# Seven tiles of scores a pair for the row maxima instead of eight, and another order of the prelude, in an attention and FFN kernel

## The chip, the cores and the metric

The kernel runs on one core of a Trainium2 chip. The metric is the device time of one execution in microseconds (us). A slot is one turn of the main loop, and a pair is two attention heads that are worked on together. Names such as PE (TensorE), DVE (VectorE), ACT (ScalarE), POOL (GpSimd) and SP (SyncE, whose queue issues all DMAs here) are those of the profile.

## What is computed

```python
q_n, k_n = rmsnorm(q, g_q), rmsnorm(k, g_k)          # 8 batches, 12 heads, 448 tokens, 64 wide
scores = matmul(q_n, k_n^T) / sqrt(64)
scores = scores - max(scores, axis=-1)
attn = exp(scores); attn = attn / (sum(attn) + 1e-9)
x = (attn @ v) laid out as 3584 tokens x 768
h = x @ w_in                                          # 768 x 2048
out = (s * relu(h)**2 + b) @ w_out                    # 2048 x 768
```

## The kernel before, in words

The 96 heads are 48 pairs (`NPAIR`), six pairs a batch. Each number is carried as a high part, rounded to the float32r type, and a low part, the rest, so that a product takes several float32r matmuls. Of a pair's tensors, `ka` holds the high part of the keys in partitions 0 to 63 (`D` = 64) and the low part in 64 to 127, and `qa` the high part of the queries twice, so one matmul of `qa` with `ka` gives nearly exact scores. `kb` and `qb` hold what is left over, and partition 64 of `qb` holds the shift, minus the maximum of each query's scores, which the second score matmul adds to the scores. Any shift near the maximum gives the same softmax, as numerator and sum are scaled alike.

The main loop (from line 895) runs over slots from `FIRST` = -22 to 384 and a few more; a pair has 8 slots (`W`), 4 for each head j, one for each block of keys. Slot s does, on each engine in the order written: the transposed scores of slot s (`score_t`, L434 and L437), two FFN matmuls, the exponential (`exponent`), then what `begun` generators have left, then the jobs that `at(slot, function, ...)` put into this slot, then the score of slot s+10 for the maxima (`score`, L396), more FFN matmuls, its maximum on DVE (`maximum`, L407), the late jobs (`convert`, `convert_out`, `invert`), and the product with the values of slot s-2 (`weigh`, L493). All engines and the SP queue take their instructions strictly in this written order.

Each of a pair's eight scores for the maxima has 112 queries, every fourth one (`c=NQ`, four columns of 112 rows), as weights against all 448 keys of its head. `shift` moves the maxima of one head by a DMA into the row of `qb`; `double_kb` copies the high keys into `kb` by a DMA.

Pairs 0 to 8 (`NR` = 9) get q and k from rows: `load_rows` (L251), `norm_rows` (ACT square L257, DVE sum L262, POOL L265 to L267), `turn` (PE transposes, L274), `split_turned` (ACT L282 to L284, DVE L286 and L287). Later pairs come by `load_kq`, `scale` and `split_kq` (ACT L377 and L378, POOL L380 and L381). `norm_rows` runs at slot s1-20, `turn` at s1-13, `split_turned` at s1-12 and its DVE half one slot later, with s1 = 8p + 4j. `double_kb` runs at s1-10 and `shift` at s1-6.

The weights `w_in` come as 64-bit floats in 24 pieces, `load_piece` (L129), and are converted by `convert` in five steps from the slots of `PACE`: DVE L133, L136, L138, L141, ACT L134 and L144, POOL L147.

During the first batch (slots 0 to 55) there is no FFN work. From slot 56 on each slot also holds six matmuls of the first FFN product (`filler`, L204) of the batch before, 288 for the 48 slots of a batch. After the last slot follow the rest of the first FFN product and the second one (L825).

Of the kernel before, what the change touches and what calls it, by code (L numbers as in the profile page):

```python
# [9 lines left out]
F32 = mybir.dt.float32  # L10
F32R = mybir.dt.float32r
I32 = mybir.dt.int32
AF = mybir.ActivationFunctionType
ALU = mybir.AluOpType
AX = mybir.AxisListType
# [14 lines left out]
FIRST = -22  # L30

FILL = (2, 2, 2)

PACE = (-18, -10, *range(1, 61, 5), *range(59, 89, 3))

GAP = 2

STEPS = {0: 2, 1: 3, 2: 4, 3: 5, 5: 6, 6: 7, 8: 8, 9: 9, 11: 10, 12: 11, 13: 12}

OUT = (92, *range(110, 141, 6), *(48 * b + i for b in range(3, 8) for i in range(14, 43, 7)))  # L40

# [2 lines left out]
def attention_then_relu2_ffn(  # L44
# [30 lines left out]
    V, S, G, T = nc.vector, nc.scalar, nc.gpsimd, nc.tensor  # L75

    NPAIR, P, _, SEQ = kq.shape
# [4 lines left out]
    D = P // 2  # L82
    NP = NPAIR // B
    H = 2 * NP
    TILES = 2 * SEQ // P
    NV = 2 * NP
    NR = rows0.shape[0]
    NQ = 4
    QC = SEQ // NQ
# [8 lines left out]
    W = 8  # L98
# [137 lines left out]
    lp = last.enter_context(tc.tile_pool(name="lpool", bufs=1, side="right"))  # L236
    ap = early.enter_context(tc.tile_pool(name="apool", bufs=1))
    if True:
        raws, kqs, invs, vrs, nmxs, shs, tks = ({} for _ in range(7))
        sts, movers, avs, uzs, zts, zbs, us = ({} for _ in range(7))  # L240
# [12 lines left out]
        def norm_rows(p, j):  # L253
            raw = raws[p, j].rearrange("p t c d -> p (t c) d")
            n = 2 * NQ
            sq = lp.tile([QC, n, D], F32, tag="al", bufs=2, name=f"sq{p}_{j}")
            S.activation(  # L257
                sq.rearrange("p i d -> p (i d)"), raw.rearrange("p i d -> p (i d)"), AF.Square
            )
            yield  # L260
            ssq = ap.tile([QC, n], F32, tag="ssq", bufs=2, name=f"ssq{p}_{j}")
            V.tensor_reduce(out=ssq, in_=sq, op=ALU.add, axis=AX.X)  # L262
            yield
            ri = ap.tile([QC, n], F32, tag="ri", bufs=2, name=f"ri{p}_{j}")
            G.tensor_scalar(ri, ssq, 1.0 / D, 1e-6, ALU.mult, ALU.add)  # L265
            G.tensor_tensor(ri, ri, mhalf[:QC, :n], ALU.pow)
            G.tensor_tensor(raw, raw, ri.unsqueeze(2).broadcast_to([QC, n, D]), ALU.mult)  # L267
# [11 lines left out]
        def split_turned(p, j):  # L279
            n, a = p % 2, slice(j * SEQ, (j + 1) * SEQ)  # L280
            (k, k_bank), (q, q_bank) = (tks.pop((p, j, t)) for t in range(2))
            S.copy(ka[n][:D, a], k)  # L282
            S.activation(qa[n][:D, a], q, AF.Copy, scale=gqk[:D])
            S.activation(qa[n][D:, a], q, AF.Copy, scale=gqk[:D])  # L284
            yield
            V.tensor_tensor(ka[n][D:, a], k, ka[n][:D, a].bitcast(F32), ALU.subtract)  # L286
            V.scalar_tensor_tensor(  # L287
                qb[n][:D, a], q, gqk[:D], qa[n][:D, a].bitcast(F32), ALU.mult, ALU.subtract
            )
            free.extend((k_bank, q_bank))  # L290
# [5 lines left out]
        def warm_up(n):  # L296

            to, bank = psum("warmth")
            for _ in range(n):
                T.matmul(to[:, :P], ident, ident, start=True, stop=True)  # L300
            free.append(bank)
# [61 lines left out]
        ka = [ap.tile([P, 2 * SEQ], F32R, name=f"ka{n}") for n in range(2)]  # L363
        qa = [ap.tile([P, 2 * SEQ], F32R, name=f"qa{n}") for n in range(2)]
        kb = [ap.tile([P, 2 * SEQ], F32R, name=f"kb{n}") for n in range(2)]
        qb = [ap.tile([P, 2 * SEQ], F32R, name=f"qb{n}") for n in range(2)]
        for t in qb:
            G.memset(t[D:P].bitcast(F32), 0.0)
        for t in kb:
            G.memset(t[D:P].bitcast(F32), 0.0)  # L370
            G.memset(t[D : D + 1].bitcast(F32), 1.0)

        def split_kq(p, j):

            t, n = kqs.pop((p, j)), p % 2
            a = slice(j * SEQ, (j + 1) * SEQ)
            S.copy(ka[n][:, a], t[:, 0])  # L377
            S.copy(qa[n][:, a], t[:, 1])  # L378
            yield
            G.tensor_tensor(ka[n][D:, a], t[D:, 0], ka[n][D:, a].bitcast(F32), ALU.subtract)  # L380
            G.tensor_tensor(qb[n][:D, a], t[:D, 1], qa[n][:D, a].bitcast(F32), ALU.subtract)  # L381

        def move(to, of):
            nc.sync.dma_start(to.bitcast(F32), of.bitcast(F32))
# [5 lines left out]
        def score(i):  # L390

            p, c = divmod(i, W)
            j, c = divmod(c, NQ)
            sh, bank = psum(f"sh{i}")
            a = slice(j * SEQ, (j + 1) * SEQ)
            T.matmul(  # L396
                sh[:QC, :SEQ], qa[p % 2][:, a].rearrange("k (p c) -> k c p", c=NQ)[:, c],
                ka[p % 2][:, a], start=True, stop=True,
            )
            shs[i] = sh, bank  # L400

        def maximum(i):
            p, c = divmod(i, W)
            if c == 0:
                nmxs[p] = ap.tile([QC, W], F32R, tag="nmx", bufs=2, name=f"nmx{p}")
            sh, bank = shs.pop(i)
            V.tensor_reduce(  # L407
                out=nmxs[p][:, c : c + 1], in_=sh[:QC, :SEQ], op=ALU.max, axis=AX.X, negate=True
            )
            free.append(bank)  # L410

        def shift(p, part):

            to = qb[p % 2][D : D + 1, part * SEQ : (part + 1) * SEQ]
            move(
                to.rearrange("o (p c) -> o p c", c=NQ), nmxs[p][:, part * NQ : (part + 1) * NQ]
            )
            if part:
                nmxs.pop(p)

        def chunk(i):
            p, g = divmod(i, W)
# [96 lines left out]
        def divide(p, step):  # L519

            if step == 1:
                nc.sync.dma_start(z_d[p].rearrange("j (p c) -> (j p) c", c=TILES), zts.pop(p))
            elif step == 2:
                zb = zbs[p] = lp.tile([P, SEQ], F32, tag="zb", name=f"zb{p}")
                for j in range(2):
                    nc.sync.dma_start(
                        zb[j * D : (j + 1) * D], z_d[p][j : j + 1].broadcast_to([D, SEQ])
                    )
            else:
                zb = zbs.pop(p)  # L530
                u = us[p] = lp.tile([P, SEQ], F32, tag="u", bufs=NP, name=f"u{p}")
                for j in range(2):
                    a = slice(j * D, (j + 1) * D)
                    G.tensor_tensor(u[a], uzs.pop((p, j))[a], zb[a], ALU.mult)  # L534
# [96 lines left out]
        def at(s_, f, *a):  # L631
            jobs[s_].append((f, a))

        for p in range(NPAIR):
            s0 = W * p
            if p >= NR:
                at(s0 - 32, load, p)
                at(s0 - 28, norm, p)
                at(s0 - 24, keep, p)
            for j in range(2):  # L640
                s1 = s0 + 4 * j
                if p >= NR:
                    at(s1 - 19, load_kq, p, j)
                    at(s1 - 19, spread, p, j)
                    at(s1 - 15, scale, p, j)
                    at(s1 - 13, split_kq, p, j)
                else:
                    at(max(s1 - 28, FIRST), load_rows, p, j)
                    at(s1 - 20, norm_rows, p, j)
                    at(s1 - 13, turn, p, j)  # L650
                    at(s1 - 12, split_turned, p, j)
                at(s1 - 10, double_kb, p, j)
                at(s1 - 6, shift, p, j)
                at(s1 + 6, take, p, j)
                at(s1 + 7, gather, p, j)
            at(s0 - (9 if p >= NV else 5), load_v, p)
            if p >= NV:
                at(s0 - 3, split_v, p)
            at(s0 + 13, invert, p)
            at(s0 + 14, divide, p, 1)  # L660
            at(s0 + 16, divide, p, 2)
            at(s0 + 18, divide, p, 3)
        for b in range(B):
            for g in range(NP):
                at(end(b + 1) - (2 if b < B - 1 else 4) + g, split_x, b, g)
        for _ in range(2):
            at(FIRST + 1, load_piece)
        for s_ in PACE:
            for n in range(5):
                at(s_ + n, convert, n)  # L670
# [218 lines left out]
        with tc.manual_schedule(engines=ORDERED):  # L889
            begun = []  # L890
            for s_ in range(FIRST, NSLOT + LAST + 2):
# [4 lines left out]
                    )  # L896
                for f, *of in drain.get(s_ - NSLOT, ()):
                    f(*of)
                if s_ == FIRST:
                    nc.sync.dma_start(gg, g_qk)  # L900
                    V.scalar_tensor_tensor(gqk, gg[:, 0:1], D**-0.5, gg[:, 1:2], ALU.mult, ALU.mult)
                if s_ == 0:
                    for t, x in ((sb_s, s), (sb_b, b_)):
                        nc.sync.dma_start(t, x.rearrange("(o d) -> o d", o=1).broadcast_to([P, 1]))
                if s_ == FIRST:
                    warm_up(30)
                if within(s_):
                    score_t(s_)
                filler(FILL[0])
# [40 lines left out]
            for n in range(NFC - 2):  # L950
# [4 lines left out]
                if n in STEPS:  # L955
                    k = STEPS[n]
# [86 lines left out]
```

## Time and profile before

| | us |
|---|---|
| median of 3 runs | 1417.05 |
| lowest and highest run | 1415.51, 1417.28 |
| the profiled execution, whole | 1414.78 |
| its span in the profile | 1412.3 |
| PE busy in the span | 1383.9 |
| DVE, POOL, ACT busy in the span | 1051.4, 1034.5, 867.5 |

The profiled execution is 2.27 us under the median, and 2.48 us of it lie outside the span. The busy shares are averages over three stages that are limited by different engines, so the text below reads them by stretches of time: the views by windows give, for each stretch, the busy time of each engine and in brackets its instructions.

### The profile page before, as it was taken

To read this page: it belongs to the slowest core of one execution; us is meant where nothing else is said; L and a number is where in the kernel's file an instruction comes from. 1 tells how busy PE (TensorE), PEld (TensorE's weight loads), DVE (VectorE), ACT (ScalarE), POOL (GpSimd) and SP (SyncE) were. 2 spreads that over 40 slices of the span, in tenths; PEclk is the share of its full clock that TensorE was granted. 3 is DMA by queue.
4 is the path that set the end of the run, shared out by engine and by line. 5 is a ranking of instruction groups with operands and counts; after the bars stand their busy time and mean duration, and the time that the engine had idled before them with its cause. 6 is when DMAs were issued, how large, how long until landed. Compare 5 with 4: busy or idle time off the path is not lost.

```text
span 1412.3 us, 22187 instructions
## 1 busy us (share of the span) xinstructions
PE 1383.9 (98%) x6996; PEld 1264.1 (90%) x6996; DVE 1051.4 (74%) x1594; ACT 867.5 (61%) x1649; POOL 1034.5 (73%) x941
## 2 busy tenths in 40 slices
PE   6989999999999999999999999999999999999999
PEld 5666788899899899999989989989999999999998
DVE  7998996887878788688788778655766666666655
ACT  5777555777777777777777777644554444544443
POOL 7778888877778777777787777267776776577663
PEclk9999999999999999999999999999999999999999
DMA  4456787677777677677767766354433333343331
GB/s 137 134 149 174 215 245 221 205 222 236 204 229 223 198 225 227 197 216 232 219 187 238 215 209 195 90 159 144 127 98 111 102 97 95 90 120 97 96 95 63
DMA packets 209252, 237.94 MB, mean 168 GB/s; under 512 B 72848, under 2 KB 187024, under 8 KB 209136
## 3 DMA queue, kind: packets, MB, share of 16 engines
q1 hardware_dynamic: 209136, 236.54, 56.7%
q8 instruction: 55, 0.90, 0.3%
q14 instruction: 61, 0.50, 0.1%
HBM read 178.00 MB, written 47.11 MB: 159 GB/s over the span
## 4 chain that ended last, share of the span: by engine, by line
PE 90%; DVE 5%; DMA 2%; issue 1%; ACT 1%; POOL 1%; SPq 0%; DVEq 0%; ACTq 0%; POOLq 0%
PE ph L204 31%; PE m L825 29%; PE av L493 14%; PE sh L396 5%; PE st L434 5%; PE st L437 5%; DVE wai L136 1%; DVE nmx L407 1%; DVE wai L133 1%; PE tk L274 1%; DVE x L542 1%; DMA zb<-z_d 0%; DMA w64i<-in_dram 0%; DVE wai L138 0%; DVE ka L286 0%
## 5 line engine op out<-in xcount | busy, mean ns | idle before, releaser
L204 PE MATMUL ph<-x,wih 128*128 128x448 f32 x1536 | 491.5, 366 | 0.5 <-DVE x L542 0.5
L825 PE MATMUL m<-t,gh 128*128 128x384 f32 x1568 | 399.3, 335 | 1.8 <-ACT ot L852 1.4
L204 PEld LDWEIGHTS ph<-x,wih 128*128 128x128 f32 x1536 | 288.7, 188 | 31.5 <-issue 7.8
L204 PE MATMUL ph<-x,wil 128*128 128x448 f32 x768 | 296.1, 386 | 0.0
L407 DVE TENSOR_REDUCE nmx<-sh 112x1 fp32r<-112x448 f32 x384 | 236.2, 617 | 79.3 <-PE sh L396 77.1
L825 PEld LDWEIGHTS m<-t,gh 128*128 128x128 f32 x1568 | 283.1, 188 | 3.1 <-ACT ot L852 1.7
L453 ACT ACTIVATE st<-st 128x448 f32<-128x448 f32 (+1 forms) x288 | 151.1, 525 | 186.9 <-PE st L437 184.0
L825 PE MATMUL m<-t,gl 128*128 128x384 f32 x784 | 262.5, 335 | 0.0
L806 ACT CAST gh<-g 128x896 fp32r<-128x896 f32 x112 | 105.8, 945 | 213.9 <-POOL g L796 156.5
L807 DVE TENSOR_TENSOR gl<-g,gh 128x896 fp32r<-128x896 f32 x112 | 130.3, 1164 | 135.7 <-ACT gh L806 133.4
L792 POOL TENSOR_TENSOR g<-g 128x256 f32<-128x256 f32 x112 | 94.7, 846 | 127.1 <-DVE g L791 127.1
L493 PE MATMUL av<-ah,vs 128*128 128x448 f32 x576 | 164.9, 367 | 0.8 <-DVE al L474 0.5
L396 PE MATMUL sh<-ka,qa 128*112 128x448 f32 x384 | 146.9, 385 | 17.3 <-DVE ka L286 12.0
L204 PEld LDWEIGHTS ph<-x,wil 128*128 128x128 f32 x768 | 144.2, 188 | 18.9 <-issue 7.9
L534 POOL TENSOR_TENSOR u<-uz,zb 64x448 f32<-64x448 f32 x96 | 134.6, 1403 | 34.6 <-DMA zb<-z_d 27.9
L434 PE MATMUL st<-qa,ka 128*128 128x448 f32 (+1 forms) x384 | 157.6, 410 | 1.4 <-ACT e L449 0.8
L461 ACT CAST ah<-st 128x448 fp32r<-128x448 f32 (+1 forms) x288 | 153.6, 533 | 1.3
L825 PEld LDWEIGHTS m<-t,gl 128*128 128x128 f32 x784 | 147.1, 188 | 0.0
L474 DVE TENSOR_TENSOR al<-st,ah 128x448 fp32r<-128x448 f32 x216 | 132.7, 614 | 18.7 <-ACT ah L461 15.8
L437 PE MATMUL st<-qb,kb 128*128 128x448 f32 (+1 forms) x384 | 140.2, 365 | 0.0
L380 POOL TENSOR_TENSOR ka<-kq,ka 64x448 fp32r<-64x448 f32 x78 | 97.8, 1253 | 52.6 <-ACT ka L377 49.2
L396 PEld LDWEIGHTS sh<-ka,qa 128*112 128x112 f32 x384 | 107.4, 280 | 30.3 <-ACT wih L144 5.4
(85 smaller groups left out, 2437.9 us busy)
## 6 DMA issues: line engine op xcount, KB each, us to landing
kq<-in_dram SPq DMA_DIRECT2D x78, 448.0 KB, 4.9
rb<-i_d SPq DMA_DIRECT2D x78, 448.0 KB, 6.0
r_d<-r SPq DMA_DIRECT2D x128, 224.0 KB, 3.1
raw<-in_dram SPq DMA_DIRECT2D x39, 448.0 KB, 4.8
raw<-r_d SPq DMA_DIRECT2D x64, 256.0 KB, 2.8
w64i<-in_dram SPq DMA_DIRECT2D x24, 512.0 KB, 4.6
w64o<-in_dram SPq DMA_DIRECT2D x32, 384.0 KB, 5.1
kb<-ka SPq DMA_DIRECT2D x96, 112.0 KB, 3.3
```

Source lines behind the costliest of these rows:

```text
L204: T.matmul(ph[:, :SEQ], w[:, cc, f0 : f0 + P], xs[b, cc][:, part, :], start=n == 0, stop=n == 3 * NCC - 1,)
L396: T.matmul(sh[:QC, :SEQ], qa[p % 2][:, a].rearrange("k (p c) -> k c p", c=NQ)[:, c], ka[p % 2][:, a], start=True, stop=True,)
L407: V.tensor_reduce(out=nmxs[p][:, c : c + 1], in_=sh[:QC, :SEQ], op=ALU.max, axis=AX.X, negate=True)
L434: T.matmul(st[:rows, :SEQ], ka[n][:, keys], qa[n][:, q], start=True, stop=False)
L437: T.matmul(st[:rows, :SEQ], kb[n][:, keys], qb[n][:, q], start=False, stop=True,)
L453: S.activation(st[:rows, :SEQ], st[:rows, :SEQ], AF.Exp)
L461: S.copy(ah[:rows], sts[i][0][:rows, :SEQ])
L474: V.tensor_tensor(al, st[:rows, :SEQ], ah[:rows].bitcast(F32), ALU.subtract)
L493: T.matmul(av[:, :SEQ], x, a, start=kc == 0 and m == 0, stop=kc == 3 and m == len(todo) - 1,)
L534: G.tensor_tensor(u[a], uzs.pop((p, j))[a], zb[a], ALU.mult)
L807: V.tensor_tensor(gl, g9[:, 1:8], gh.bitcast(F32), ALU.subtract)
L825: T.matmul(to, g[:, sa], w, start=m == 0 and n == 0, stop=m == NM - 1 and n == 2,)
```

## The change

The scores for the maxima are laid out otherwise. Of each head's 448 queries 384 (`FULL`) go into three tiles of 128 (every third query, `c=NF`), and the last 64 of both heads share a seventh tile: `both_q` has head 0's in its first 64 partitions and columns and head 1's in the others, with zeros elsewhere, and `both_k` has the high keys of head 0 in partitions 0 to 63 and of head 1 in 64 to 127. `UNITS` says which slot of a pair scores what: slots 0, 1, 2 head 0, slot 4 the shared tile, slots 5, 6, 7 head 1, slot 3 nothing. `both_k` is written by a DMA (`stack_k`, slot s0-10) and by a new ACT copy in `split_turned` and `split_kq` for j = 1; `both_q` by two ACT copies (`stack_q`, slot s0-7). The maxima of the shared tile get two DMAs of their own (`shift_rest`, slots s0-5 and s0-3).

In the prelude the order of loads, the first conversion's slot, the memsets' engine and the number of warming matmuls change. Two temporary tiles get other buffers.

```diff
-PACE = (-18, -10, *range(1, 61, 5), *range(59, 89, 3))
+PACE = (-15, -10, *range(1, 61, 5), *range(59, 89, 3))
+UNITS = {0: (0, 0), 1: (0, 1), 2: (0, 2), 4: (2, 0), 5: (1, 0), 6: (1, 1), 7: (1, 2)}
...
+    NF = SEQ // P
+    FULL = NF * P
...
-            sq = lp.tile([QC, n, D], F32, tag="al", bufs=2, name=f"sq{p}_{j}")
+            sq = ap.tile([QC, n, D], F32, tag="vr", name=f"sq{p}_{j}")
...
             S.copy(ka[n][:D, a], k)
+            if j:
+                S.copy(both_k[D:], k)
...
-        for t in qb:
-            G.memset(t[D:P].bitcast(F32), 0.0)
-        for t in kb:
-            G.memset(t[D:P].bitcast(F32), 0.0)
-            G.memset(t[D : D + 1].bitcast(F32), 1.0)
+        for E, n in ((V, 0), (G, 1)):
+            for t in (qb[n], kb[n]):
+                E.memset(t[D:P].bitcast(F32), 0.0)
+            E.memset(kb[n][D : D + 1].bitcast(F32), 1.0)
+
+        both_k = ap.tile([P, SEQ], F32R, name="both_k")
+        both_q = ap.tile([P, P], F32R, name="both_q")
+        G.memset(both_q.bitcast(F32), 0.0)
+
+        def stack_k(p):
+            move(both_k[:D], ka[p % 2][:D, :SEQ])
+
+        def stack_q(p):
+            for j in range(2):
+                a = slice(j * D, (j + 1) * D)
+                S.copy(both_q[a, a], qa[p % 2][a, j * SEQ + FULL : (j + 1) * SEQ])
...
             S.copy(qa[n][:, a], t[:, 1])
+            if j:
+                S.copy(both_k[D:], t[D:, 0])
...
-            j, c = divmod(c, NQ)
+            if c not in UNITS:
+                return
+            j, c = UNITS[c]
             sh, bank = psum(f"sh{i}")
-            a = slice(j * SEQ, (j + 1) * SEQ)
-            T.matmul(
-                sh[:QC, :SEQ], qa[p % 2][:, a].rearrange("k (p c) -> k c p", c=NQ)[:, c],
-                ka[p % 2][:, a], start=True, stop=True,
-            )
+            if j < 2:
+                a = slice(j * SEQ, (j + 1) * SEQ)
+                T.matmul(
+                    sh[:, :SEQ],
+                    qa[p % 2][:, a][:, :FULL].rearrange("k (p c) -> k c p", c=NF)[:, c],
+                    ka[p % 2][:, a], start=True, stop=True,
+                )
+            else:
+                T.matmul(sh[:, :SEQ], both_q, both_k, start=True, stop=True)
...
             V.tensor_reduce(
-                out=nmxs[p][:, c : c + 1], in_=sh[:QC, :SEQ], op=ALU.max, axis=AX.X, negate=True
+                out=nmxs[p][:, u : u + 1], in_=sh[:, :SEQ], op=ALU.max, axis=AX.X, negate=True
             )
...
+            nmx, row = nmxs[p], qb[p % 2][D : D + 1, part * SEQ : (part + 1) * SEQ]
             move(
-                to.rearrange("o (p c) -> o p c", c=NQ), nmxs[p][:, part * NQ : (part + 1) * NQ]
+                row[:, :FULL].rearrange("o (p c) -> o p c", c=NF),
+                nmx[:, part * NF : (part + 1) * NF],
             )
+        def shift_rest(p, part):
+            to = qb[p % 2][D : D + 1, part * SEQ + FULL : (part + 1) * SEQ]
+            move(to.rearrange("o (p c) -> o p c", c=1), nmxs[p][part * D : (part + 1) * D, 2 * NF :])
...
-                u = us[p] = lp.tile([P, SEQ], F32, tag="u", bufs=NP, name=f"u{p}")
+                of = dict(tag="al", bufs=2) if p == NPAIR - 1 else dict(tag="u", bufs=NP - 1)
+                u = us[p] = lp.tile([P, SEQ], F32, name=f"u{p}", **of)
...
-                    at(max(s1 - 28, FIRST), load_rows, p, j)
+                    at(max(s1 - 28, FIRST + j), load_rows, p, j)
...
+            at(s0 - 10, stack_k, p)
+            at(s0 - 7, stack_q, p)
+            at(s0 - 5, shift_rest, p, 0)
+            at(s0 - 3, shift_rest, p, 1)
...
-        for _ in range(2):
-            at(FIRST + 1, load_piece)
+        for s_ in (FIRST, FIRST + 3):
+            at(s_, load_piece)
...
-                if s_ == FIRST:
+                if s_ == FIRST + 2:
                     nc.sync.dma_start(gg, g_qk)
+                if s_ == FIRST + 4:
                     V.scalar_tensor_tensor(gqk, gg[:, 0:1], D**-0.5, gg[:, 1:2], ALU.mult, ALU.mult)
...
-                    warm_up(30)
+                    warm_up(20)
```

More of the change, by code (lines that the diff above doesn't have):

```diff
@@ L404, in maximum @@
             if c == 0:
-                nmxs[p] = ap.tile([QC, W], F32R, tag="nmx", bufs=2, name=f"nmx{p}")
+                nmxs[p] = ap.tile([P, 2 * NF + 1], F32R, tag="nmx", bufs=2, name=f"nmx{p}")
+            if c not in UNITS:
+                return
+            j, c = UNITS[c]
             sh, bank = shs.pop(i)
+            u = j * NF + c
             V.tensor_reduce(
-                out=nmxs[p][:, c : c + 1], in_=sh[:QC, :SEQ], op=ALU.max, axis=AX.X, negate=True
+                out=nmxs[p][:, u : u + 1], in_=sh[:, :SEQ], op=ALU.max, axis=AX.X, negate=True
             )
@@ L412, in shift @@
         def shift(p, part):
-            to = qb[p % 2][D : D + 1, part * SEQ : (part + 1) * SEQ]
+            nmx, row = nmxs[p], qb[p % 2][D : D + 1, part * SEQ : (part + 1) * SEQ]
             move(
-                to.rearrange("o (p c) -> o p c", c=NQ), nmxs[p][:, part * NQ : (part + 1) * NQ]
-            )
-            if part:
-                nmxs.pop(p)
+                row[:, :FULL].rearrange("o (p c) -> o p c", c=NF),
+                nmx[:, part * NF : (part + 1) * NF],
+            )
+        def shift_rest(p, part):
+            to = qb[p % 2][D : D + 1, part * SEQ + FULL : (part + 1) * SEQ]
+            move(to.rearrange("o (p c) -> o p c", c=1), nmxs[p][part * D : (part + 1) * D, 2 * NF :])
         def chunk(i):
```

## The prediction

> **What bounds the kernel now.** I read the page first, then the busy times by stretches, then the chain in order of time, to find where each engine sets the pace.
>
> ```profile
> span 1412.3 us, 22187 instructions
> PE 1383.9 (98%) x6996; PEld 1264.1 (90%) x6996; DVE 1051.4 (74%) x1594; ACT 867.5 (61%) x1649; POOL 1034.5 (73%) x941
> PE ph L204 31%; PE m L825 29%; PE av L493 14%; PE sh L396 5%; PE st L434 5%; PE st L437 5%; DVE wai L136 1%; DVE nmx L407 1%; DVE wai L133 1%; PE tk L274 1%; DVE x L542 1%; DMA zb<-z_d 0%; DMA w64i<-in_dram 0%; DVE wai L138 0%; DVE ka L286 0%
> ```
>
> Over the whole span PE is the bound, and the scores for the maxima (sh) hold 5% of the chain. The stretches separate the stages; I cut them at the first transposed score of slot 0 and where the chain passes from DVE to PE for good (second fence). The third row counts only L434, one per slot.
>
> ```profile
> 0.00:26.70 26.70, 16.71 (x102) 14.99 (x103) 17.38 (x28) 12.06 (x20) 21.19 (x29) 0.94 0.52 146
> 26.70:150.60 123.90, 112.27 (x471) 78.66 (x470) 112.52 (x183) 89.06 (x174) 99.37 (x93) 1.00 0.56 153
> 150.60:917.00 766.40, 765.34 (x3685) 688.85 (x3686) 612.30 (x993) 539.93 (x1104) 583.12 (x439) 1.00 0.71 212
> 26.70:150.60 123.90, 40.68 (x64) 11.94 (x64) 1.00 0.56 153
> ```
>
> ```profile
> 149.97 0.55 DVE nmx L407
> 150.56 0.56 PE sh L396
> ```
>
> From 150.6 to 917 us PE is busy 765.34 of 766.40: nothing but fewer matmuls helps there, and anything another engine gains is lost. From 26.7 to 150.6 (slots 0 to 63) DVE and PE are both busy about 91%, and up to 150.56 the chain keeps returning to DVE. Before 26.7 it is a prelude of loads and first conversions.
>
> **The steady stage, slots 64 to 383.** The price of one matmul there is the distance between starts, not its duration.
>
> ```profile
> 491.01 0.36 PE L204 MATMUL ph<-x,wih 128*128 128x448 f32 x1
> 491.21 0.37 PE L204 MATMUL ph<-x,wil 128*128 128x448 f32 x1
> 491.42 0.36 PE L396 MATMUL sh<-ka,qa 128*112 128x448 f32 x1
> ```
>
> They start every 0.205 us, though each is recorded with 0.36 (their ends overlap). Slot s scores unit s+10, so slots 64 to 383 hold units 74 to 383; among them is unit 3 of pairs 9 to 47, 39 matmuls. 39 x 0.205 = **8.0 us** go, provided the remaining ones stay as cheap. Their weights become 128 columns, one float in three, where they were 112, one in four.
>
> ```profile
> 26.97 0.28 PEld L396 LDWEIGHTS sh<-ka,qa 128*112 128x112 f32 x1
> 27.17 0.37 PE L396 MATMUL sh<-ka,qa 128*112 128x448 f32 x1
> 27.37 0.36 PE L434 MATMUL st<-qa,ka 128*128 128x448 f32 x1
> ```
>
> A strided load takes 0.28 us now, more than the 0.205 between starts, and yet the next matmul starts 0.20 after: it lies under the matmuls in flight. In proportion to columns 128 would take 0.32. The extra cost lies between 0 and 0.04 a tile (six tiles, 39 pairs: 0 to 9.4 us); I take 0, as the present load beyond the spacing costs nothing. The Trainium skill ("TensorE: Matmul & The Clock Gate", LDWEIGHTS (loading the stationary operand), and Back-to-back issue gap) has a load's time grow with its columns and the spacing set by load and matmul together; this trace agrees with neither its figure, 107 ns for 128 columns, nor so far with a spacing that a longer load stretches.
>
> Beside PE, the change adds ACT work: a copy of 64x448 and two of 64x64 a pair.
>
> ```profile
> L282 ACT CAST ka<-tk 64x448 fp32r<-64x448 f32 x18 | 9.3, 516 | 2.6 <-PE tk L274 2.6
> L735 ACT CAST t<-w 128x192 fp32r<-128x192 f32 x16 | 5.6, 350 | 0.9 <-POOL w L727 0.4
> ```
>
> The first costs 0.52; a small one lies between 0 and 0.35, I take 0.25: 1.0 us a pair, 39 us in the stage. ACT is busy 540 of 766 us, so it fits; what is behind a copy (exponentials, splits) feeds `weigh` two slots later, nearly 5 us. The three added DMAs are 112 KB and two of 64 single floats a pair; 112 KB every 19 us is 6 GB/s beside 212. They land long before their readers (below, for the tight stage). Cost 0; if the cover fails, a pair loses what the late one is late. The freed DVE time (0.62 a pair) is worth nothing here. After 917 us the change touches nothing, so that part only starts sooner.
>
> **Slots 0 to 63.** Here the removed maximum counts: unit 3 of pairs 1 to 8 (slots 1, 9 to 57), and of pair 0 in the prelude.
>
> ```profile
> L407 DVE TENSOR_REDUCE nmx<-sh 112x1 fp32r<-112x448 f32 x384 | 236.2, 617 | 79.3 <-PE sh L396 77.1
> ```
>
> A maximum is over 448 elements a row before and after, so 0.617 us each: 8 x 0.617 = 4.9 us at most (with the 0.2 of PE inside it), 0 at least if other waits fill the gaps. DVE is busy 91%, PE too, and ACT, 72% busy, gets 1.0 us a pair more. I take three quarters, **3.7 us**.
>
> What is late next? The shared tile needs `stack_k`, queued on SP right behind `double_kb` of the same slot, s0-10, and is scored at s0-6. Pair 3, s0 = 24:
>
> ```profile
> 54.21 0.55 SPq L384 DMA_DIRECT2D kb<-ka  x1
> 58.41 0.54 PE L396 MATMUL sh<-ka,qa 128*112 128x448 f32 x1 [0.66 <-DVE ka L286]
> kb<-ka SPq DMA_DIRECT2D x96, 112.0 KB, 3.3
> ```
>
> The DMA of slot 14 was issued at 54.21, after a wait in SP's queue for DVE. One behind it starts about 54.8 and lands about 58.1. The score of slot 18 stood at 58.41, held by DVE L286: the new wait ends where the old one did, and head 1's first score, which needs L286, has moved a slot later. So I cost it at 0, with 0 to 1.5 us a pair over pairs 2 to 7 as bounds. Behind that score on PE stand slot 18's `weigh` and all later matmuls; ACT's next exponential waits for those. `shift_rest` makes SP wait for the shared tile's maximum; behind it stand `load_v` and row loads, used five or more slots later.
>
> **The prelude.**
>
> ```profile
> 0.72 0.39 SPq L900 DMA_DIRECT2D gg<-in_dram  x1
> 1.16 0.89 SPq L251 DMA_DIRECT2D rows<-in_dram  x2
> 2.09 0.90 SPq L129 DMA_DIRECT2D w64i<-in_dram  x2
> 2.29 9.07 PE L300 MATMUL warmth<-ident 128*128 128x128 f32 x60 [2.29 <-POOL ident masks.py:199]
> 3.97 0.63 ACT L257 ACTIVATE sq<-rows 112x512 f32<-112x512 f32 x1 [1.76 <-DMA rows<-in_dram]
> 4.63 0.69 DVE L262 TENSOR_REDUCE ssq<-sq 112x8 f32<-112x512 f32 x1 [1.97 <-ACT sq L257]
> 4.65 1.62 POOL L371 MEMSET kb<- 1x896 f32 x2
> 6.65 1.66 POOL L266 TENSOR_TENSOR ri<-ri,mhalf 112x8 f32<-112x8 f32 x1
> 8.31 0.43 DVE L133 TENSOR_SCALAR wai<-w64i 128x512 int32<-128x512 int32 x1 [3.00 <-DMA w64i<-in_dram]
> 8.39 1.25 POOL L267 TENSOR_TENSOR rows<-rows,ri 112x512 f32<-112x512 f32 x1
> 11.20 0.93 PE L274 MATMUL tk<-ident,rows 112*64 112x112 f32 x8
> 11.64 0.68 DVE L262 TENSOR_REDUCE ssq<-sq 112x8 f32<-112x512 f32 x1
> 12.83 0.62 DVE L286 TENSOR_TENSOR ka<-tk,ka 64x448 fp32r<-64x448 f32 x1 [0.52 <-ACT ka L282]
> ```
>
> The first row load moves from 1.16 to 0.72, so its square from 3.97 to about 3.5 and the sum's end to 4.9. POOL loses three of its six 0.8 us memsets and is free at about 4 instead of 6.27; L265 to L267 took 3.27 from there, so the rows are ready at about 8.1. A third of the warming matmuls go: PE is free at 2.29 + 9.07 x 2/3 = 8.3. So the first transposes start at 8.4 instead of 11.20, 2.8 sooner. DVE's three memsets (each between 0.1 and 1.2 us: no row has one on DVE) end before 4.2; cost 0.
>
> But DVE's block of work, the first conversion and the second sum (8.31 to 12.32, 4.0 us), still comes before L286, and in the new order the sum goes first. It waits for the second rows, now behind a 512 KB piece: they land between about 4 and 8.3, the landing of that piece before. DVE then reaches L286 between 9.9 (PE's and ACT's pace) and 13.0, against 12.83: 2.9 sooner to 0.2 later. I take **2.0 us**, since the piece is itself issued 0.9 sooner and with one DMA ahead, not two. From 15 us DVE works almost without gaps, so this carries to slot 0, as does pair 0's removed maximum, **0.6 us**.
>
> A gap of PE has a price too:
>
> ```profile
> 20.75 0.70 PE L396 MATMUL sh<-ka,qa 128*112 128x448 f32 x1 [3.58 <-DVE ka L286]
> 21.25 1.70 PE L274 MATMUL tk<-ident,rows 112*64 112x112 f32 x8
> 20.00:24.00 4.00, 3.25 (x12) 2.38 (x12) 3.58 (x7) 2.13 (x4) 2.70 (x4) 0.57 0.39 124
> ```
>
> After 3.58 us idle the granted clock was 0.57, and eight transposes took 1.70 instead of 0.93. The shared tile, which needs no L286, may break this gap; the shorter warming may open another. I take 0, bounds 0.8 either way. The Trainium skill ("TensorE: Matmul & The Clock Gate", What's actually happening) gates the clock after an idle window of about 3.4 us; the trace agrees.
>
> The temporaries cost 0: the square's single buffer is read (sum ends 5.32) before the next square, and the last pair's u takes a place that no chunk needs then.
>
> **Sum.** 8.0 + 3.7 + 2.0 + 0.6 = 14.3 us. The profiled execution becomes 1414.78 - 14.3 = 1400.5; the same from the median, 1417.05, is 1402.8. I forecast **1402.0**, between them, nearer the median.
>
> **Rivals.**
> - *The shared tile waits for its DMA.* For it: SP's lag; against: the old wait ended as late. At 1.0 to 1.5 us for pairs 2 to 7 it eats 6 to 9 us: 1407 to 1411. Chance 0.13.
> - *The prelude gives nothing*, as the second rows land last: the 2.0 go, and slots 0 to 63 give half: 1404 to 1407. Chance 0.20.
> - *All of it comes*: 4.9 for the slots, 2.9 and 0.8 for the prelude: 17.2 us, 1397.5 to 1400. Chance 0.13.
> - *Slower: the longer strided weight load is exposed.* Place: L396 in the steady stage; it decides from the point at which 0.32 no longer fits under the matmuls in flight. If each of six tiles then took 0.32 instead of 0.205, a pair would lose 0.69 and save 0.205: 39 x 0.485 = 19 us lost, against 6.3 gained before: about 1429. If only part is exposed it comes out near no change. Against it: 0.28 costs nothing now. Chances 0.04 and 0.03.
> - *The removed score is covered anyway*, so that the steady stage keeps its slots of 12 matmuls' length: it would need another engine as bound, and none is busy over 80% there: 1411. Chance 0.02.
>
> **How the numbers follow.** Forecast (1400 to 1404) 0.45, rivals as above. The range 1397.5 to 1409.5 leaves out the two slow cases, the covered score and part of the waiting tile. Within 0.2% of the median, about what a measurement of this kernel tells from no change, is 1414.2 to 1419.9. Faster: 0.93; same 0.03; slower 0.04.
>
> **What the profile after would show.** Steady slots without a score 0.205 shorter, once a pair, and 39 x 0.205 less between slots 64 and 383; the spacing after an sh load still 0.20. The first transposes near 8.4, L286 near 10.8, slot 0 near 24.1 instead of 26.76, slot 63's score near 144. The forecast is wrong if PE's wait for `stack_k` shows in slots 10 to 50, if spacing around L396 is over 0.22, or if L286 stays near 13.

## The result and the profile after

The changed kernel takes 1430.88 us in the median of 4 runs (1428.79 to 1435.2), the kernel before 1417.16 in the same comparison: a ratio of 1.0102, 95% interval 1.0082 to 1.0121. It became 1.0% slower where 1.1% faster was forecast. The span grew from 1412.3 to 1427.4 us. The page of the changed kernel, its busy times and its chain:

```profile
span 1427.4 us, 22453 instructions
PE 1384.1 (97%) x6928; PEld 1256.1 (88%) x6928; DVE 1035.0 (73%) x1549; ACT 923.2 (65%) x1793; POOL 998.4 (70%) x939
PE 79%; DVE 7%; DMA 5%; ACT 4%; issue 2%; POOL 2%; SPq 1%; DVEq 0%; ACTq 0%; POOLq 0%
```

PE issued fewer matmuls and was busy as long; ACT gained 56 us. ACT holds 4% of the chain (the work that ended last, followed back), where it held 1%. Where the 15 us came from shows when the first transposed score of a slot starts, before (L434) and after (L466); the timeline has the start in its first column. Slots 0, 55, 104 and 383 of the kernel after:

```profile
24.65 0.57 PE L466 MATMUL st<-qa,ka 128*128 128x448 f32 x1
...
138.37 0.71 PE L466 MATMUL st<-qa,ka 128*128 128x448 f32 x1
...
267.26 0.36 PE L466 MATMUL st<-qa,ka 128*128 128x448 f32 x1
...
931.86 0.36 PE L466 MATMUL st<-qa,ka 128*64 128x448 f32 x1
```

The same slots of the kernel before, of which slot 0 stood at 26.76 in the stretch cut there (26.70):

```profile
125.93 0.47 PE L434 MATMUL st<-qa,ka 128*128 128x448 f32 x1 [0.45 <-DMA w64i<-in_dram]
...
254.87 0.37 PE L434 MATMUL st<-qa,ka 128*128 128x448 f32 x1
...
916.52 0.36 PE L434 MATMUL st<-qa,ka 128*64 128x448 f32 x1
```

| stage | before | after | difference |
|---|---|---|---|
| start to slot 0 | 26.76 | 24.65 | -2.1 |
| slot 0 to 55 | 99.17 | 113.72 | +14.6 |
| slot 55 to 104 | 128.94 | 128.89 | 0.0 |
| slot 104 to 383 | 661.65 | 664.60 | +3.0 |
| slot 383 to the end of the span | 495.78 | 495.54 | -0.2 |

The prelude gained. Nearly all the loss lies in the first batch, and the steady stage, which was to bring 8 us, lost three from slot 104 on. Each has its own cause in the trace.

**Slots 0 to 55.** Three rows of the waits of the whole run (waiting instruction, what released it, us in total, times, longest; PEld is the weight load, which waits in the same gaps as its matmul):

```profile
PEld sh L424 <- ACT both_q L388: 21.1, 8, 3.1
PE sh L424 <- ACT both_q L388: 15.2, 7, 2.5
PE sh L424 <- DMA w64i<-in_dram: 2.5, 1, 2.5
```

L424 is the shared tile's score. It waits for ACT's second copy into `both_q`, and not for the DMA into `both_k`. The third row is one more such gap, though it names a DMA of `w64i`, which the score does not read: there the copies into `both_q` ran from 62.68 to 63.18 us, and the score started at 63.24. One of these gaps in the timeline, ACT's line ahead of it and what follows on PE:

```profile
43.75 0.63 ACT L289 ACTIVATE qa<-tk,gqk 64x448 fp32r<-64x448 f32 x1
44.39 0.63 ACT L290 ACTIVATE qa<-tk,gqk 64x448 fp32r<-64x448 f32 x1
45.05 0.63 ACT L261 ACTIVATE sq<-rows 112x512 f32<-112x512 f32 x1
45.58 0.53 ACT L481 ACTIVATE e<-st 128x448 f32<-128x448 f32 x1
46.00 0.50 ACT L388 CAST both_q<-qa 64x64 fp32r<-64x64 f32 x2
...
46.55 0.47 PE L424 MATMUL sh<-both_k,both_q 128*128 128x448 f32 x1 [1.92 <-ACT both_q L388]
...
48.25 1.70 PE L278 MATMUL tk<-ident,rows 112*64 112x112 f32 x8
```

Without pause ACT works through two copies into `qa`, the next square, an exponential and only then `both_q`. PE stands 1.92 us, then its transposes take 1.70 us where eight took 0.93: its clock had fallen. Read in windows of half a us, the granted clock is still 1.00 at 47.5 and 0.50 from 48.0 to 51.0. By stretches from 30 to 130 us, first before, then after:

```profile
30.00:130.00 100.00, 91.19 (x386) 62.79 (x385) 92.17 (x154) 74.45 (x147) 80.26 (x77) 1.00 0.53 143
```

```profile
30.00:130.00 100.00, 84.95 (x330) 58.18 (x330) 78.99 (x129) 72.09 (x146) 63.65 (x67) 0.91 0.46 123
```

DVE, the bound here before, fell from 92 to 79 us busy, PE from 91 to 85, and the granted clock to 0.91. No engine is full: the stage has become one of waits.

**Slots 104 to 383.** Slots 113, 114 and 115, first before, then after:

```profile
277.02 0.36 PE L434 MATMUL st<-qa,ka 128*128 128x448 f32 x1
279.25 0.36 PE L434 MATMUL st<-qa,ka 128*128 128x448 f32 x1
281.69 0.36 PE L434 MATMUL st<-qa,ka 128*64 128x448 f32 x1
```

```profile
290.98 0.36 PE L466 MATMUL st<-qa,ka 128*128 128x448 f32 x1
293.00 0.36 PE L466 MATMUL st<-qa,ka 128*128 128x448 f32 x1
295.43 0.37 PE L466 MATMUL st<-qa,ka 128*64 128x448 f32 x1
```

Slot 113 has no score any more and takes 2.02 us instead of 2.23, and 114 keeps 2.43: 0.21 gained, as forecast. But slots 104 to 106, at the end of a batch, take 3.88, 2.34 and 3.05 us (by the starts of L466) instead of 2.66, 2.47 and 2.57. Between slots 104 and 383 there are 34 slots without a score: -7.0 us. The stage lost 3.0, so six ends of batches cost 9.9 us, about 1.65 each. One of them:

```profile
382.69 0.56 ACT L397 CAST both_k<-kq 64x448 fp32r<-64x448 f32 x1
383.26 0.57 ACT L574 CAST x<-u 128x448 fp32r<-128x448 f32 x1
383.86 1.15 DVE L575 TENSOR_TENSOR x<-u,x 128x448 fp32r<-128x448 f32 x1 [1.93 <-ACT x L574]
384.94 0.61 DVE L506 TENSOR_TENSOR al<-st,ah 128x448 fp32r<-128x448 f32 x1
385.61 0.47 PE L208 MATMUL ph<-x,wih 128*128 128x448 f32 x1 [0.55 <-DVE al L506]
```

Here ACT also splits `x`; with the 0.56 us copy into `both_k` ahead of it DVE waits 1.93 us, is late with the splits behind, and PE waits for DVE.

### The profile page after: what moved, and what is told of

Its sections match the earlier page's. It is cut to its first block, busy times and chain, and to the rows that moved or that the text cites. A ratio compares the mean times of both kernels' runs of the same rounds, so it can differ in the third digit from the quotient of the medians.

```text
span 1427.4 us, 22453 instructions
## 1 busy us (share of the span) xinstructions
PE 1384.1 (97%) x6928; PEld 1256.1 (88%) x6928; DVE 1035.0 (73%) x1549; ACT 923.2 (65%) x1793; POOL 998.4 (70%) x939
## 4 chain that ended last, share of the span: by engine, by line
PE 79%; DVE 7%; DMA 5%; ACT 4%; issue 2%; POOL 2%; SPq 1%; DVEq 0%; ACTq 0%; POOLq 0%
PE m L862 29%; PE ph L208 26%; PE av L525 12%; PE st L466 4%; PE st L469 4%; PE sh L418 3%; DVE x L575 2%; DMA qb<-nmx 2%; DMA w64i<-in_dram 1%; PE tk L278 1%; DVE nmx L436 1%; DVE kq L365 1%; DVE al L506 1%; PE sh L424 1%; DMA zt<-uz 1%
## 5 line engine op out<-in xcount | busy, mean ns | idle before, releaser
L436 DVE TENSOR_REDUCE nmx<-sh 128x1 fp32r<-128x448 f32 x336 | 207.3, 618 | 60.0 <-PE sh L418 51.9
L829 POOL TENSOR_TENSOR g<-g 128x256 f32<-128x256 f32 x112 | 97.5, 870 | 127.7 <-DVE g L828 127.7
L567 POOL TENSOR_TENSOR u<-uz,zb 64x448 f32<-64x448 f32 x96 | 119.0, 1240 | 64.7 <-DMA zb<-z_d 61.8
L466 PE MATMUL st<-qa,ka 128*128 128x448 f32 (+1 forms) x384 | 161.3, 420 | 1.9 <-ACT e L481 1.2
L399 POOL TENSOR_TENSOR ka<-kq,ka 64x448 fp32r<-64x448 f32 x78 | 94.8, 1216 | 58.8 <-ACT ka L394 55.6
L833 POOL TENSOR_TENSOR g<-g 128x256 f32<-128x256 f32 x112 | 123.5, 1103 | 0.0
L418 PE MATMUL sh<-ka,qa 128*128 128x448 f32 x288 | 111.9, 391 | 8.2 <-DVE ka L292 4.0
```

The source lines that it names most:

```text
L418: T.matmul(sh[:, :SEQ], qa[p % 2][:, a][:, :FULL].rearrange("k (p c) -> k c p", c=NF)[:, c], ka[p % 2][:, a], start=True, stop=True,)
L436: V.tensor_reduce(out=nmxs[p][:, u : u + 1], in_=sh[:, :SEQ], op=ALU.max, axis=AX.X, negate=True)
L466: T.matmul(st[:rows, :SEQ], ka[n][:, keys], qa[n][:, q], start=True, stop=False)
L833: G.tensor_tensor(g9[:, 5:7], g9[:, 0:9:8], g9[:, 1:8:6], ALU.subtract)
```

## The experiments

The lines of code differ a little from kernel to kernel, so the same instruction has other numbers in each. Slot 55 stands at 125.93 before and 138.37 after.

**1. The wait alone taken away.**

```diff
-            at(s0 - 7, stack_q, p)
+            at(s0 - (5 if p else 7), stack_q, p)
...
-                S.copy(both_q[a, a], ...)
+                S.activation(both_q[a, a], ..., AF.Copy, scale=64.0)
```

> The two ACT copies into both_q stay, but from pair 1 on they stand two slots later, behind the score of the shared tile that reads both_q. So that score no longer waits for them, and it sees the queries of the pair before, times 64 (the outputs of the last 64 queries of a head are wrong in this kernel). Theory A (the score of the shared tile waits for the last of a row of ACT copies, and PE stands still in slots 0 to 55): slot 55 comes 10 to 14 us sooner than after the change (138.4 there), the whole time falls to 1416 to 1420. Theory B (the wait is for the DMA into both_k, stack_k): PE waits just as long, the name of the releaser changes, slot 55 stays within 2 us of 138 and the time near 1430. Theory C (the clock of PE alone, from the shorter warming): no change either.

1418.55 us, ratio 1.0016 (0.9999 to 1.0032). Slots 0 and 55:

```profile
25.14 0.57 PE L468 MATMUL st<-qa,ka 128*128 128x448 f32 x1
...
121.22 0.47 PE L468 MATMUL st<-qa,ka 128*128 128x448 f32 x1 [0.36 <-ACT e L483]
```

With the same number of ACT copies, slots 0 to 55 take 96.1 us instead of 113.7, and 3.1 less than before the change. So the wait and what follows from it cost 17.6 us, and the ACT work as such nothing that shows there. Theories B and C fall. Slot 55 comes 17.2 us sooner, more than the 10 to 14 forecast, and slots 104 to 383 take 671.0 us instead of 664.6 in the profiled executions; as the two misses offset each other, the time lies in the range given for it by luck. The edit moved the ACT copies in that stage too, but that this made it slower was not tested.

**2. The gap filled, not removed.**

```diff
+            if 0 < p < NR:
+                at(s0 - 6, warm_up, 6)
```

> Six matmuls without use (128 columns, 0.3 us each as two passes) stand ahead of the shared tile's score of pairs 1 to 8, where PE is idle 2 to 3 us. The wait stays. Theory A1 (of the 2.3 us that a pair of slots 0 to 55 loses about half is the wait and half the clock that falls to 0.5 after it): transposes after the gap take 0.93 instead of 1.70, the granted clock from 20 to 60 us rises from about 0.6 to over 0.8, and the time falls by 4 to 8 us, to 1423 to 1427. Theory A2 (the wait is all): the clock rises, the time stays within 2 us of 1430.

1423.75 us, ratio 1.0061 (1.0039 to 1.0083), in theory A1's range. From 30 to 130 us the granted clock is 1.00, the eight transposes take 0.93 us each time, and slot 55 stands at 131.66:

```profile
30.00:130.00 100.00, 91.49 (x430) 66.17 (x429) 84.31 (x135) 77.14 (x155) 71.08 (x73) 1.00 0.51 136
...
131.66 0.71 PE L466 MATMUL st<-qa,ka 128*128 128x448 f32 x1
```

From slot 0 (24.43) to 55 it is 107.2 us against 113.7 with the change and 96.1 in the first run. So of the 17.6 us that the wait costs, about 6.5 come through the clock and 11.1 from the gaps themselves; the 14.6 us lost to the kernel before are less, because the removed score gains 3.1 once nothing waits. Theory A1 holds, with a somewhat smaller share for the clock. The expectation's clock of about 0.6 from 20 to 60 us was misread: the change has 0.82 there and this run 0.91.

**3 and 4. Seven tiles only where they gain.** A function `seven(p)` chooses per pair between the old eight tiles and the new seven, with their copies and DMAs.

```diff
+        def seven(p):
+            return p >= NR                      # third run
+            return p >= NR and p % NP != 2      # fourth run
```

> Pairs 0 to 8, those that come by rows, get eight tiles as before the change; pairs 9 to 47 keep seven. The prelude is the changed one. Theory A: slots 0 to 55 lose their stall but also the gain of the maxima, so slot 56 stands about 2 us before that of the kernel before (126 against 128.0); after it the stalls at the ends of batches stay. The time is about 1414 to 1418, a ratio of 0.998 to 1.000 to the kernel before. If the loss came from the prelude or its clock instead, it stays near 1428.

> As the run before, and also the pairs whose ACT copies fall into the slots in which ACT splits x at the end of a batch (every sixth, from pair 14) get eight tiles. Theory D (after slot 104 the gain of 0.2 us a pair is real, and 1.2 to 1.9 us at each of six ends of a batch, where ACT is late with x and with the splits, eat it): 8 to 10 us less than the run before, 1404 to 1409, ratio about 0.992 to 0.994, and slots 104 to 107 of a batch's end take 2.65, 2.47, 2.57 as in the kernel before. Rival theory (the stalls at the ends come from the five buffers of u instead of six, or from the added DMAs): the same stalls stay, and the time is that of the run before.

The third takes 1418.03 us, ratio 1.0013 (1.0003 to 1.0023), at the upper edge of its range, with slot 55 at 124.47, 1.5 us before that of the kernel before: the prelude's gain is kept and slots 0 to 55 lose nothing. Slots 104 to 383 take 666.2 us against 661.7 before, so the ends of batches cost more than the steady stage gains. The fourth takes 1408.29, ratio 0.9951 (0.9936 to 0.9967), as forecast; slots 104 to 106 take 2.66, 2.48 and 2.57. Theory D's place is right. The five buffers of u are unchanged in it, so they are not the cause; the added DMAs, which left with the tiles, are judged by the eleventh run.

**5. The prelude alone** (`seven(p)` never true).

> Eight tiles for every pair; of the change stay the prelude's order, the memsets, the shorter warming, the other buffers of two temporaries (and the unused tiles both_k and both_q). The two mixed runs show slot 0 1.8 to 2.0 us sooner and 1.4 to 1.5 left from slot 4 on. So 1.4 us in all: ratio 0.998 to 1.000, time 1415 to 1416. If five buffers of u instead of six hold anything up, the ends of batches show it here, and the time is above that of the kernel before.

1414.41 us, ratio 0.9985 (0.9976 to 0.9994), a little better than expected: slots 0 and 55 stand at 24.10 and 123.68, 2.7 and 2.3 us before those of the kernel before. The third and fourth run have the same work up to slot 0 and reach it at 25.01 and 24.82, so single executions differ there by nearly 1 us. The prelude of the change is a gain, and the other places of the temporaries cost nothing that shows at the ends of batches.

**6 and 7. The shared tile later**, with seven tiles for all pairs but those at the ends (`p == 2 or p % NP != 2`).

```diff
-UNITS = {..., 4: (2, 0), 5: (1, 0), 6: (1, 1), 7: (1, 2)}
+UNITS = {..., 4: (1, 0), 5: (2, 0), 6: (1, 1), 7: (1, 2)}      # sixth run, shift_rest at s0-4 and s0-3
+UNITS = {..., 4: (1, 0), 5: (1, 1), 6: (2, 0), 7: (1, 2)}      # seventh run, shift_rest at s0-3 and s0-2
```

> Seven tiles for all pairs but those at the ends of batches; the shared tile is scored one slot later, after head 1's first tile, and shift_rest of head 0 one slot later. Theory A: ACT has one slot (1.4 to 2.2 us) more for both_q, so the gap of 1.9 to 2.5 us shrinks to 0.5 us or less, and so does the loss of clock that follows it: slot 56 stands between that of the run with the wait removed (4.7 us before the kernel before) and 2 us behind the kernel before; time 1404 to 1411. Rival (the place matters less than the amount of ACT work): slot 56 stays 8 us or more behind, the time is over 1414.

> The same with the shared tile two slots later than in the change, before head 1's last tile, and both shift_rest one slot after it or two. Theory A: no wait for both_q is left, slot 56 stands 3 to 4.7 us before the kernel before, time 1404 to 1406. Rival (the wait moves on): head 0's part of the shared maxima then has three slots for its DMA of 3.5 us and for SP's lag of 3 to 6 us, and the first transposed scores of a pair in slots 0 to 55 wait for qb: 1 to 2 us a pair, time 1410 to 1416.

1409.86 (0.9958, 0.9941 to 0.9975) and 1409.95 us (0.9958, 0.9943 to 0.9972), slot 55 at 126.50 and 128.29. The time of the sixth is in theory A's wide range, that of the seventh is not: the gain of slots 0 to 55 did not come, although only one score still waits for `both_q`. The longest waits of the scores (L431) in the seventh from 24 to 150 us:

```profile
PE sh L431 <- DVE ka L292: 6.8, 4, 2.3
PEld sh L431 <- ACT qa L290: 6.3, 5, 2.2
PE sh L431 <- ACT qa L290: 3.5, 4, 1.9
PEld sh L431 <- ACT both_q L391: 2.7, 1, 2.7
```

Head 1's first tile is back in slot s0-6 and waits there for `qa` and for DVE's `ka`, as it did before the change. The rival's time nearly came, but not its cause: its wait for `qb` is one of 1.3 us. Nor is it the clock, which was 0.98 and 0.99 from 30 to 130 us in the two runs. That ACT's added copies make `qa` and `ka` later than before would explain the rest, but was only argued.

**8. DVE instead of ACT at the ends** (`V.tensor_copy` into `both_k` and `both_q` for `p % NP == 2`, seven tiles from pair 9).

> Seven tiles from pair 9 on, also at the ends of batches, where DVE instead of ACT writes both_k and both_q (pairs 14, 20, 26, ...). Theory D (at the ends it is ACT's queue that is overfull): the 1.2 to 1.9 us stalls go as they did with eight tiles there, 1406 to 1410; DVE's copies may cost a few tenths each. Rival (the slots there are too full for any engine, DVE's x and splits included): stalls of over 1 us remain, 1414 to 1418.

1416.16 us, ratio 0.9999 (0.9990 to 1.0008), in the rival's range. The stall moved from slot 104 to 106 (2.67, 2.53 and 4.37 us), where PE waits 1.4 us at most for a split by DVE. That ACT's queue alone is overfull is thereby wrong.

**9 and 10. The same ACT work in another order.** For pairs that come by rows, `both_q` is written directly from PSUM, ahead of the long copies.

```diff
             S.copy(ka[n][:D, a], k)
+            if seven(p):
+                if j:
+                    S.copy(both_k[D:], k)
+                h = slice(j * D, (j + 1) * D)
+                S.activation(both_q[h, h], q[:, FULL:], AF.Copy, scale=gqk[:D])
             S.activation(qa[n][:D, a], q, AF.Copy, scale=gqk[:D])
```

> As the runs with seven tiles for all pairs but those at the ends of batches, the shared tile in its place of the change (slot s0-6); but for the pairs that come by rows ACT writes both_q directly from PSUM, inside split_turned, ahead of the two long copies into qa instead of after them and after the next square and exponential. The amount of ACT work is the same. Theory A (it is the place of both_q in ACT's order that PE waits for): both_q is ready 2 to 3 us sooner, the gap of 1.9 to 2.5 us goes, slot 56 stands 3 to 4.7 us before the kernel before, as with the wait removed; time 1404 to 1407. Rival (any wait of PE for that row of ACT copies costs as much, wherever it stands, since ACT is the bound there): slot 56 stays behind the kernel before, time 1409 or more.

> The same, with the shared tile one slot later, behind head 1's first tile. Theory E (in the two runs with a later shared tile, head 1's first score went back to the slot where it waits for L286 and the qa copies, as in the kernel before, and that wait is what kept slot 56 behind): the time is as in the run with the shared tile fifth, 1408 to 1411, although both_q is ready sooner. Rival (what held those runs was both_q or the DMAs of shift_rest): it falls to 1404 to 1407 too.

The ninth, with the shared tile in the place of the change, takes 1404.57 us, ratio 0.9912 (0.9895 to 0.9928), in theory A's range. Its slot 55 and its waits for the two operands of the shared tile (L440) over the whole run:

```profile
123.27 0.47 PE L494 MATMUL st<-qa,ka 128*128 128x448 f32 x1 [0.79 <-ACT e L509]
```

```profile
PE sh L440 <- DMA both_k<-ka: 5.4, 5, 3.7
PEld sh L440 <- ACT both_q L291: 1.4, 2, 0.7
```

The wait for `both_q` is all but gone, and now the DMA into `both_k` shows: 3.7 us once, in the prelude, and four times 0.3 to 0.5 us after slot 0. Slot 55 stands 2.7 us before that of the kernel before, a little short of the 3 to 4.7 expected. The tenth takes 1411.78 us, ratio 0.9964 (0.9951 to 0.9977), slot 55 at 127.64: with head 1's first tile in slot s0-6, its weight load waits there for `qa` again (12.9 us of the run, 8 times), however early `both_q` is ready. The time is 0.8 us above theory E's range and far from the rival's, so theory E holds: the slot wants a tile that needs neither `qa` of both halves nor DVE's `ka`.

**11 and 12. The ends of batches again**, with the order of the ninth and seven tiles for all pairs but pair 8. For `p % NP == 2` from pair 14 on, the eleventh writes both tiles by POOL (`G.tensor_copy`), the twelfth `both_k` by a second DMA from `ka` and `both_q` by ACT.

> As the run with both_q from PSUM (1404.6), but seven tiles also for the pairs at the ends of batches, with both_k and both_q written by POOL for these pairs. Theory D1 (at the ends x goes ACT, then DVE, and work added to either of the two makes the splits that PE waits for late, while POOL is outside that chain): no stall at the ends, 0.2 us more gained at each, 1403 to 1405. Theory D2 (the slots there take no further work on any engine): stalls of over 1 us at six ends, 1411 to 1416.

> The same, with both_k's second half written by a DMA from ka for these pairs, and both_q by ACT as in the change. It tells the two ACT steps at the ends apart. Theory D1: the first stall (1.2 us, behind the 0.56 us copy into both_k) goes and the second (0.5 to 0.8 us, behind the two copies of 0.24 us into both_q) stays: 6 x 0.5 to 0.8 less 6 x 0.2, so 1406 to 1409. If the first stall came from something else of the change at the ends, the time is 1412 or more.

The eleventh takes 1404.51 us, ratio 0.9913 (0.9889 to 0.9936), as forecast by theory D1, the best of these with the ninth; slots 104 to 106 take 2.66, 2.03 and 2.83, so the gain comes at the ends too, with all of the change's DMAs in place: theory D1. The twelfth takes 1409.88, ratio 0.9948 (0.9929 to 0.9967), 0.9 us above its range: slot 104 has 2.66 again, and slot 106 and its like at the six ends have 2.99, 2.44, 3.77, 3.00, 3.00 and 3.86, up to 1.3 over the 2.57 before. The first stall was the copy into `both_k`. What remains goes with `both_q` on ACT or with the added DMA. No edit tells these two apart, but in the trace PE's waits from 250 to 915 us are for DVE's splits (4.3 us, 7 times) and for ACT's `both_q` (1.3 us, 5 times), and none is for a DMA.

## Why the prediction was wrong, point by point

- **The step that failed** is the answer to "What is late next?" in slots 0 to 63. It weighed the DMA of `stack_k` against the old wait for L286 and put its cost at 0, which was nearly right: once the ACT wait was gone, in the ninth run, that DMA cost 1.7 us in four waits after slot 0. But the shared tile also waits for `stack_q`, whose two copies stand in ACT's order behind four others, a square and the exponentials, and this wait was given no term at all. In the steady part the text held that what is behind a copy feeds `weigh` two slots later; the copies' own reader one slot later was left out. In place of 3.7 us gained, slots 0 to 55 lost 14.6; against the first run the wait costs 17.6, of which 6.5 come through the clock.
- **The term of 3.7 us** for the removed maximum stands at 3.1 in the first run, whose shared tile reads the queries of the pair before. In the ninth, which reads the right ones and has seven tiles for pairs 0 to 7, slots 0 to 55 take 98.1 us, only 1.1 less than before the change.
- **The clock** was bounded at 0.8 us either way, for one gap in the prelude. It fell after five of the seven gaps between slots 0 and 55 (last section).
- **The steady stage.** 0.205 us a slot without a score came as forecast from slot 98 on, and the weight load of 128 strided columns stays covered: it takes 0.25 us, not the 0.32 that the forecast scaled up from 112 columns, the score's slot kept its length, and the slower rival did not occur. What failed is "Cost 0" for ACT, taken from 540 busy of 766 us: an average. At six ends of batches, where `x` goes through ACT and DVE, the copies cost 1.65 us each, 9.9 against 7.0 gained. That it is a chain over two engines and not ACT's load alone shows in the eighth and the eleventh run: DVE instead of ACT hardly helps, POOL does.
- **Slots 64 to 98** gained nothing, for a cause that stays open (last section).
- **The prelude.** Slot 0 was forecast near 24.1 and stood at 24.65; the first transposes at 8.4 against 8.98, as POOL's product of the rows took 1.84 us where it had taken 1.25; L286's successor (L292) at 10.8 against 10.91. This is right, also in that the second rows were not last: the square of them began at 6.22. The 0.6 us for pair 0's removed maximum does not show: the third, fourth and fifth run, with eight tiles for pair 0, reach slot 0 at 25.01, 24.82 and 24.10.
- **The range** ended at 1409.5, as the slower rivals were priced from loads and DMAs alone. None of them was the one that came, and none of the forecast's signs of being wrong was the wait for `both_q`.

The change can pay: with `both_q` early in ACT's order and the ends of batches relieved, the same idea takes 1404.5 us, 12.6 below the kernel before in that comparison (1417.1), against 14.3 forecast.

## What to carry to other kernels

When a change gives an instruction a new operand, list every producer of it and the place of each in its engine's queue; the last of them counts, and a short copy behind five long ones is late though its engine is not full. An idle share of an engine over a stage says nothing about the slots in which its work gathers: price added work in the fullest slot, along the chain that passes through it. A gap on PE that returns once a pair costs its length and, where the clock falls after it, more than half as much again (6.5 beside 11.1 us here).

## What the runs showed that was not expected

- Gaps on PE of 1.9 to 2.5 us were enough to lower the granted clock. In windows of half a us, five of the seven gaps at the shared tile between slots 0 and 55 (2.54, 1.92, 2.44, 1.90 and 2.20 us) are followed by about 3.4 us at 0.50. After the other two (2.48 and 1.90 us), and after the gaps of up to 1.73 us in the kernel before, it stays at 1.00, so the length of a gap alone does not decide; what does was not tested. Eight transposes take up to 1.70 us in such a stretch instead of 0.93. The forecast had leaned on one gap of 3.58 us. The Trainium skill ("TensorE: Matmul & The Clock Gate", What's actually happening) names an idle window of about 3.4 us; here shorter gaps did it, and the measurement decides.
- The changed prelude runs at a lower clock: the granted clock is 0.50 from 14 to 26 us, where before it fell only from 20 to 24 us (0.60 and 0.55 in windows of 2 us). All twelve experiments have such a stretch, of about 7 to 14 us. The forecast put the prelude's clock at 0, with bounds of 0.8 us, and whether the shorter warming brings this stretch was not tested.
- In slots 64 to 98 with seven tiles, every slot but the one without a score takes 2.60 us instead of 2.57, and that one 2.40: 0.03 a slot, 0.24 a pair, which cancels the 0.205 gained there. It shows in the fourth run too and not in the fifth, so it goes with the seven tiles; it ends at slot 98, where the products with the values change form. What causes it was not tested.
- Copies added on DVE at the ends of batches cost nearly as much as on ACT (1416.16 against 1418.03 us), on POOL nothing that shows.
